# Local and global value products regrouped in a fused attention and feed-forward kernel on one core

## The chip, the cores and the metric

One core of one Trainium2 chip. The time is device microseconds of one execution; the kernel before has a median of 1009.82 us over 3 runs (1008.92 to 1010.57).

## The reference

Two stages. The first is attention with 8 batches, 8 heads, 512 local and 32 global positions and head size 64; local positions see the global ones and a window of 32 to each side, global positions see all. The second is a feed-forward layer on the 4608 tokens of 512 channels, 2048 wide inside.

```python
k_all = concat([k_g, k_l]); v_all = concat([v_g, v_l])
s_g = scale * q_g @ k_all.T
out_g = softmax(s_g) @ v_all
s_ll = where(abs(i - j) <= 32, scale * q_l @ k_l.T, -1e9)
s_lg = scale * q_l @ k_g.T
out_l = softmax(concat([s_lg, s_ll])) @ concat([v_g, v_l])
x = concat([out_g, out_l])            # tokens x 512
h = maximum(x @ w_in, 0)
out = (s * h * h + b) @ w_out
```

All inputs are float32.

## The kernel before

The work is laid out in steps `j` (the loop at L582). A step takes one head of one half of a batch (256 local rows): 16 steps are one batch, 128 steps are all heads. Each half batch gives one tile of 256 tokens with all 512 channels; the feed-forward layer of a tile is 8 steps `m`, each with two blocks of 128 inner channels, and runs 10 steps behind the attention (`m = j - LAG`). Tile 16, the last, holds the global rows of all batches, which travel through a DRAM tile `xg_d`.

Most products are made in float32r (one pass of the array) from operands split into a high and a low part: ScalarE casts the high part, VectorE or GpSimd subtracts it to get the low part. A plain float32 matmul takes no split; it shows in the trace as two records, each with its own weight load.

In a step, in TensorE's order: the scores of head `j` (`scores`, four matmuls at L351 and one for the global queries at L363); in odd steps the local value products of the two heads `j-3` and `j-2` (`pv`, L318, float32, the two heads in the lower and upper 64 columns of the array); the first feed-forward product of step `m` (`ffn_in`, 24 matmuls at L493); in some steps the global value product (`g_pv`, L443); the second feed-forward product of step `m-1` (`ffn_out`, 12 matmuls at L528), with the transposes of the global probabilities (`g_transposes`, L417) between its halves where they are due. At the last step of a tile's eight (`m % 8 == 7`) the next tile is split into `xs` (`x_split`, L464 on ScalarE and L465 on VectorE), behind that step's first product; `xs` has one buffer, and `ffn_in` of the next step reads it, channel block by channel block, each with the products high x high, weight-high x x-low and weight-low x x-high.

The local path of a head: scores, softmax on VectorE and ScalarE (L207, L214, L217 to L223), copies to `two` (L384), a DMA transpose issued by SyncE (L386), a copy `join` on ScalarE one step later (L394), then `pv`, whose result ScalarE copies to the tile `x` (L325). `pt`, which `join` writes, and `rv`, the values, have two buffers each, one per pair of heads.

The global path of four heads (half the heads of a batch, `g`): `g_softmax` at step 16b+12 or 16b+16; three steps later the transposes, whose result is split by ScalarE (L421) and VectorE (L422) into `pg`; V comes in two loads of 320 KB (`g_load`, L427), is split by ScalarE (L434) and GpSimd (L435) into `vsg`; then two products `g_pv` for two heads each, one and three steps behind the transposes, of 10 matmuls with 64 output columns (32 queries, high and low) and 128 moving columns (64 values, high and low). ScalarE copies (L447) and VectorE adds (L448, L451) the parts.

From step 18 on (`ORDERED`), TensorE, ScalarE and VectorE run in the order of the program text (`manual_schedule`); GpSimd, SyncE's queue and everything before step 18 are ordered by the framework's scheduler. The 8 first head pairs (steps 0 to 15) take another path with float32 products throughout, beside the loading and splitting of the weights (`weight_chunk`), which use the buffers `pg` and `vsg` too. The eight banks of PSUM have the tags s, g, t, o, h (two), acc0 and acc1; `pv` uses o, `g_pv` t.

Of the kernel before, what the change touches and what calls it, by code (L numbers as in the profile page):

```python
# [10 lines left out]
F32 = mybir.dt.float32  # L11
F32R = mybir.dt.float32r
# [9 lines left out]
P = 128  # L22
# [22 lines left out]
NF = 16  # L45
# [8 lines left out]
X_ACT = lambda i: i >= 4  # L54
G_AT = (12, 16)
G_TR = 3
G_LD = (0, 2)
G_PV = (1, 3)
GL_POOL = lambda m: False
K_POOL = lambda j: True  # L60

# [1 line left out]
def f32(ap):  # L63
    return ap.bitcast(F32)
# [3 lines left out]
def window_attention_then_ffn(ctx: ExitStack, tc: tile.TileContext, qd, qp, qg, kw, vw, vg, w_in, w_out, sv, bv, out):  # L68
# [214 lines left out]
    def chunks(j):  # L283
        b, hf, h = slot(j)
        o = 0
        for blk in range(2):
            for c in range(2):
                c0, q0, n = CHUNKS[hf, blk][c]
                yield blk, c, c0, q0, n, slice(o, o + n)
                o += n  # L290
# [18 lines left out]
            list(p_transposes(j))  # L309
            nc.scalar.copy(out=pt[:, n, 0:NC], in_=st_.pop(("pst", j)))  # L310

    def pv(i):
        pt, rv = st_.pop(("ptp", i)), st_.pop(("rvp", i))
        p_o = ps.tile([P, 2, 2, P], F32, tag="o", name=f"ps_op{i}")
        for blk, c, c0, q0, n, o in sorted(chunks(2 * i), key=lambda x: (x[0], -x[1])):
            v = (2 * blk + c) * D
            for k in range(2):
                nc.tensor.matmul(  # L318
                    p_o[64 * k:64 * k + 64, 0, blk, q0:q0 + n], lhsT=rv[:, k, v:v + D],
                    rhs=pt[:, k, o] if i < NF // 2 else pt[:, k, 2 * blk + c, q0:q0 + n],  # L320
                    start=(c == 1), stop=(c == 0),
                )
        x_out = x_tile(2 * i)[:, i % 4, :].rearrange("p (k q) -> p k q", k=2)
        if X_ACT(i):
            nc.scalar.copy(out=x_out, in_=p_o[:, 0])  # L325
        else:
            nc.vector.tensor_copy(out=x_out, in_=p_o[:, 0])

    def qg_load(b):
        rqg = sb.tile([P, 264], F32, tag="xr", name=f"rqg{b}", bufs=1)[:, 0:H * SG]  # L330
# [78 lines left out]

    def g_transposes(b, g):  # L410
        sg = st_["sg", b, g]
        pg = st_["pg", b, g] = sb.tile([P, 5, 4, 2, SG], F32R, tag="pg", name=f"pg{b}_{g}", bufs=1)
        for c0, c1, tag in ((0, 4, "t"), (4, 5, "o")):
            p_t = ps.tile([P, 4, P], F32, tag=tag, name=f"ps_tg{b}_{g}_{c0}")
            for c in range(c0, c1):
                s0 = min(c * P, SGW - P)
                nc.tensor.transpose(out=p_t[:, c - c0, :], in_=sg[:, s0:s0 + P], identity=ident)  # L417
            v = p_t[:, 0:c1 - c0].rearrange("p c (h q) -> p (c h) q", h=4)
            ph, pl = (pg[:, c0:c1, :, i, :].rearrange("p c h q -> p (c h) q") for i in range(2))
            with tc.high_priority():  # L420
                nc.scalar.copy(out=ph, in_=v)  # L421
                nc.vector.tensor_sub(out=pl, in0=v, in1=f32(ph))  # L422
            yield

    def g_load(b, h):
        rv = st_["rvg", b, h] = sb.tile([P, 10 * D], F32, tag="rvg", name=f"rvg{b}_{h}", bufs=1)
        nc.sync.dma_start(rv, vg[b, h // 2])  # L427

    def g_split(b, h):
        rv = st_.pop(("rvg", b, h))  # L430
        vs = sb.tile([P, 2, 5, 2, D], F32R, tag="vsg", name=f"vsg{b}_{h}", bufs=1)
        for i in range(2):
            rv5 = rv[:, 5 * D * i:5 * D * (i + 1)].rearrange("p (c d) -> p c d", d=D)
            nc.scalar.copy(out=vs[:, i, :, 0, :], in_=rv5)  # L434
            nc.gpsimd.tensor_sub(out=vs[:, i, :, 1, :], in0=rv5, in1=f32(vs[:, i, :, 0, :]))  # L435
        st_["vsg", b, h] = vs

    def g_pv(b, h):
        pg, vs = st_["pg", b, h // 4], st_.pop(("vsg", b, h))
        p_g = ps.tile([P, 512], F32, tag="t", name=f"ps_og{b}_{h}")  # L440
        for i in range(2):
            for c in range(5):
                nc.tensor.matmul(  # L443
                    p_g[0:64, i * P:(i + 1) * P], lhsT=pg[:, c, h % 4 + i], rhs=vs[:, i, c], start=(c == 0), stop=(c == 4),
                )
        t = sb.tile([32, 2 * P + 40], F32, tag="og", name=f"og{b}_{h}", bufs=1)[:, 0:2 * P]
        nc.scalar.copy(out=t, in_=p_g[32:64, 0:2 * P])  # L447
        nc.vector.tensor_add(out=t, in0=p_g[0:32, 0:2 * P], in1=t)  # L448
        xr = sb.tile([P, 264], F32, tag="xr", name=f"xr{b}_{h}", bufs=1)[0:32, 0:2 * D]
        t = t.rearrange("q (h a d) -> q h a d", h=2, a=2)  # L450
        nc.vector.tensor_add(out=xr.rearrange("q (h d) -> q h d", h=2), in0=t[:, :, 0], in1=t[:, :, 1])  # L451
        nc.sync.dma_start(xg_d[b * SG:(b + 1) * SG, h * D:(h + 2) * D], xr)


    NT = 17
# [28 lines left out]
    def ffn_in(m, then):  # L484
        t, pr = m // 8, m % 8
        xs = xs_[t]
        p_h = ps.tile([P, 2, HALF], F32, tag="h", name=f"ps_h{m}", bufs=2)
        for k in range(2):
            f = 2 * pr + k
            n = 0  # L490
            for c in range(4):
                for a, e in ((0, 0), (0, 1), (1, 0)):
                    nc.tensor.matmul(  # L493
                        p_h[:, k], lhsT=wi[f][:, a, c, :], rhs=xs[:, e, c, :],
                        start=(n == 0), stop=(n == 11),
                    )
                    n += 1
# [49 lines left out]

    ENGINES = {getattr(mybir.EngineType, e) for e in ("PE", "Activation", "DVE")}
    NM = NT * 8
    early, extra, turns = defaultdict(list), defaultdict(list), {}  # L550
    for b in range(B):
        for g in range(2):
            s0 = 16 * b + G_AT[g]
            early[s0].append(lambda b=b, g=g: g_softmax(b, g))
            turns[s0 + G_TR] = g_transposes(b, g)
            for i in range(2):
                h = 4 * g + 2 * i
                early[s0 + G_TR + G_LD[i] - 1].append(lambda b=b, h=h: g_load(b, h))
                early[s0 + G_TR + G_LD[i]].append(lambda b=b, h=h: g_split(b, h))
                extra[s0 + G_TR + G_PV[i]].append(lambda b=b, h=h: g_pv(b, h))  # L560

    def pick(pair, split_one):
        def run(j):
# [18 lines left out]
    for j in range(NM + LAG + 2):  # L582
        if j == ORDERED:
            fixed.enter_context(tc.manual_schedule(engines=ENGINES))
        sp(j + 1)
        if j + 4 < NF:
            ld(j + 4)
        if j + 2 >= NF:
            ld(j + 2)
        if NF <= j < NS and j % 2 == 0:  # L590
            v_load(j // 2)
        for _ in range(CHUNKS_AT[j] if j < len(CHUNKS_AT) else 0):
            weight_chunk(chunk)
            chunk += 1
        if j < NS:
            b1 = j // 16 + 1
            if j % 16 == 14 and b1 < B:
                qg_load(b1)
            sc(j)
            if j % 16 == 15 and NF <= j + 1 < NS:  # L600
                qg_split(b1)
        tr(j - 1)
        pvs(j - 2)
        if NF <= j - 3 < NS and j % 2:
            pv((j - 3) // 2)
# [10 lines left out]
        then = extra.pop(j, [])  # L616
# [16 lines left out]
    assert chunk == 16 and not extra and not early  # L633


# [73 lines left out]
```

## Time and profile before

| | |
|---|---|
| median of 3 runs | 1009.82 us |
| the profiled execution's own time | 1010.45 us |
| its span, first to last instruction | 1008.0 us |
| TensorE busy | 969.8 us, 96% |
| ScalarE busy | 744.2 us, 74% |
| VectorE busy | 688.1 us, 68% |
| GpSimd busy | 274.7 us, 27% |
| mean granted TensorE clock | 0.977 |

A profile row names the line, the engine, the operation and its tiles (out<-in), the part of the array used (rows*columns), the shape that is streamed, the count, and after the bar the busy time, the mean duration of one, and the idle time of the engine before them with what ended it. PE is TensorE's matmuls, PEld its weight loads, DVE VectorE, ACT ScalarE, POOL GpSimd, SP SyncE. Matmuls are pipelined: a bar lasts longer than the distance to the next one's start.

### The profile page before, as it was taken

The page shows a single profiled execution, that of the slowest core. Times are in us where ns is not written, and L with a number is a line of the kernel's source. Part 1 is how long each engine was busy: PE and PEld are TensorE (multiplying, and loading weights), DVE is VectorE, ACT ScalarE, POOL GpSimd, SP SyncE. Part 2 cuts the span into 40 slices and gives each one's busy share as a digit, 9 for nine tenths or more (in the row PEclk, how much of TensorE's full clock was granted, in tenths as well). Part 3 has the DMA queues.
Part 4 walks back from the last instruction along what each step waited for, and adds up shares of the span by engine and source line. Part 5 has one row for each costly group of instructions (what it writes and reads, how often), then busy time and mean ns, then how long its engine had stood idle before and what let it go on. Part 6 is the DMA issues. An engine that isn't in the chain of part 4 may idle for free.

```text
span 1008.0 us, 19973 instructions
## 1 busy us (share of the span) xinstructions
PE 969.8 (96%) x7060; PEld 861.2 (85%) x7060; DVE 688.1 (68%) x2092; ACT 744.2 (74%) x1618; POOL 274.7 (27%) x309
## 2 busy tenths in 40 slices
PE   6879999999999999999999999999999999999996
PEld 2468889998899888998999889998999889999895
DVE  5999866776767767777767767777767777753321
ACT  5987787778888787878877787787878787853221
POOL 1011332233323342233323342233323232211000
PEclk8769999999999999999999999999999999999998
DMA  8953254444544454444444454445544454331000
GB/s 323 349 185 99 67 137 109 114 105 120 126 112 100 104 137 107 112 110 122 123 114 101 98 143 99 118 105 132 119 115 102 120 120 88 84 60 36 12 21 21
DMA packets 179627, 115.07 MB, mean 114 GB/s; under 512 B 124744, under 2 KB 166728, under 8 KB 179528
## 3 DMA queue, kind: packets, MB, share of 16 engines
q1 hardware_dynamic: 179240, 112.76, 43.4%
q8 instruction: 55, 0.90, 0.4%
q10 hardware_dynamic: 288, 1.05, 0.4%
q14 instruction: 44, 0.36, 0.1%
HBM read 74.97 MB, written 9.44 MB: 84 GB/s over the span
## 4 chain that ended last, share of the span: by engine, by line
PE 48%; ACT 17%; DVE 10%; issue 2%; DVEq 0%; ACTq 0%
PE acc L528 21%; PE ps_h L493 20%; ACT sm L214 3%; DVE r L502 3%; PE ps_op L318 3%; ACT ptp L394 3%; ACT g L509 3%; PE ps_s L351 2%; ACT kq L191 2%; DVE two L384 1%; DVE xs L465 1%; ACT kq L193 1%; ACT tg L371 1%; PE ps_og L443 1%; ACT vsg L434 1%
## 5 line engine op out<-in xcount | busy, mean ns | idle before, releaser
L493 PE MATMUL ps_h<-xs,w 128*128 128x256 f32 x3264 | 420.9, 284 | 8.3 <-DVE xs L465 6.0
L493 PEld LDWEIGHTS ps_h<-xs,w 128*128 128x128 f32 x3264 | 397.7, 190 | 20.7 <-DVE xs L465 8.0
L528 PE MATMUL acc<-w,g 128*128 128x512 f32 x1632 | 403.3, 395 | 0.0
L528 PEld LDWEIGHTS acc<-w,g 128*128 128x128 f32 x1632 | 295.0, 188 | 57.4 <-issue 0.5
L192 POOL TENSOR_TENSOR kq<-rk,kq 64x416 fp32r<-64x416 f32 x112 | 125.3, 1119 | 550.7 <-ACT kq L191 537.5
L509 ACT ACTIVATE g<-r,b_t 128x512 fp32r<-128x512 f32 x136 | 98.4, 724 | 126.5 <-DVE r L502 126.5
L510 DVE SCALAR_TENSOR_TENSOR g<-r,b_t,g 128x512 fp32r<-128x512 f32 x136 | 102.1, 751 | 102.9 <-ACT g L509 102.9
L394 ACT COPY ptp<-turned 128x1024 int16<-128x1024 int16 x112 | 152.5, 1362 | 1.7 <-DMA turned<-two 1.7
L502 DVE SCALAR_TENSOR_TENSOR r<-ps_h,s_t,r 128x512 f32<-128x512 f32 x136 | 101.3, 745 | 68.0 <-ACT r L501 66.1
L214 ACT ACTIVATE sm<-sm,nm 128x224 f32<-128x224 f32 (+1 forms) x256 | 117.7, 461 | 3.1 <-DVE nm L207 1.1
L501 ACT ACTIVATE r<-ps_h 128x512 f32<-128x512 f32 x136 | 81.4, 599 | 47.4 <-PE ps_h L493 45.0
L384 DVE COPY two<-sm 128x256 int16<-128x256 int16 x448 | 100.5, 287 | 0.0
L194 POOL TENSOR_TENSOR kq<-rq,kq 128x256 fp32r<-128x256 f32 x112 | 84.4, 753 | 8.8
L435 POOL TENSOR_TENSOR vsg<-rvg,vsg 128x320 fp32r<-128x320 f32 x64 | 56.5, 904 | 89.2 <-ACT vsg L434 89.2
L207 DVE CUSTOM_DVE_ANT_0 sm<-ps_s,mask 128x192 f32<-128x192 f32 (+1 forms) x224 | 74.2, 368 | 7.0 <-PE ps_s L351 6.8
L351 PEld LDWEIGHTS ps_s<-kq 128*128 128x128 f32 x448 | 71.7, 189 | 7.0 <-DVE nm L207 0.2
L351 PE MATMUL ps_s<-kq 128*128 128x192 f32 (+1 forms) x448 | 77.7, 265 | 0.0
L217 DVE TENSOR_SCALAR ss<-ss 128x2 f32<-128x2 f32 (+1 forms) x120 | 37.4, 312 | 45.6 <-ACT sm L214 45.5
L223 DVE TENSOR_SCALAR sm<-sm,ss 128x192 f32<-128x192 f32 (+1 forms) x224 | 65.7, 336 | 3.9
L318 PE MATMUL ps_op<-ptp,rvp 128*64 128x128 f32 (+2 forms) x1024 | 66.4, 266 | 1.5 <-ACT ptp L310 1.4
L318 PEld LDWEIGHTS ps_op<-ptp,rvp 128*64 128x64 f32 x1024 | 53.3, 141 | 13.3 <-ACT ptp L310 3.6
L372 DVE TENSOR_TENSOR sg<-ps_g,tg 32x256 f32<-32x256 f32 (+1 forms) x112 | 48.2, 431 | 20.7 <-ACT tg L371 17.3
(68 smaller groups left out, 803.9 us busy)
## 6 DMA issues: line engine op xcount, KB each, us to landing
rvp<-in_vw SPq DMA_DIRECT2D x64, 256.0 KB, 2.9
rq<-in_qd SPq DMA_DIRECT2D x112, 128.0 KB, 2.3
rk<-in_kw SPq DMA_DIRECT2D x56, 208.0 KB, 2.4
rvg<-in_vg SPq DMA_DIRECT2D x32, 320.0 KB, 3.0
out<-o SPq DMA_DIRECT2D x34, 256.0 KB, 3.0
wst<-in_w_in SPq DMA_DIRECT2D x15, 512.0 KB, 6.1
wst<-in_w_out SPq DMA_DIRECT2D x15, 512.0 KB, 6.7
turned<-two SPq DMA_TRANSPOSE x112, 3.1
```

The lines of the kernel that those rows point to most:

```text
L192: (nc.gpsimd if K_POOL(j) else nc.vector).tensor_sub(out=ks[p1:p1 + 64], in0=rk[p0:p0 + 64], in1=f32(ks[p0:p0 + 64]))
L194: nc.gpsimd.tensor_sub(out=qs[:, 1, :], in0=rq, in1=f32(qs[:, 0, :]))
L214: nc.scalar.activation(out=p, in_=p, func=AF.Exp, bias=nm[:, n:n + 1], scale=-1.0, accum_out=ss[:, n:n + 1],)
L318: nc.tensor.matmul(p_o[64 * k:64 * k + 64, 0, blk, q0:q0 + n], lhsT=rv[:, k, v:v + D], rhs=pt[:, k, o] if i < NF // 2 else pt[:, k, 2 * bl ...
L351: nc.tensor.matmul(p_s[:, cols], lhsT=qs[:, a, blk * P:(blk + 1) * P], rhs=ks[:, cols], start=(a == 0), stop=(a == 1),)
L384: nc.vector.tensor_copy(out=two[:, 2 * blk + c], in_=sm[:, :, c0:c0 + P])
L394: nc.scalar.copy(out=pt.bitcast(I16).rearrange("p c (q h) -> p c h q", h=2), in_=st_.pop(("turned", j)))
L493: nc.tensor.matmul(p_h[:, k], lhsT=wi[f][:, a, c, :], rhs=xs[:, e, c, :], start=(n == 0), stop=(n == 11),)
L502: nc.vector.scalar_tensor_tensor(out=r, in0=p_h, scalar=s_t, in1=r, op0=ALU.mult, op1=ALU.mult)
L509: nc.scalar.activation(out=g[:, 0], in_=r, func=AF.Identity, bias=b_t)
L510: nc.vector.scalar_tensor_tensor(out=g[:, 1], in0=r, scalar=b_t, in1=f32(g[:, 0]), op0=ALU.add, op1=ALU.subtract,)
L528: nc.tensor.matmul(oacc[t][i], lhsT=g[:, a, k, i * P:(i + 1) * P], rhs=wo[f][:, e, :], start=(pr == 0 and n == 0), stop=(pr == 7 and n == 5),)
```

## The change

Local value products: `pv` takes two pairs of heads at once, at every fourth step (`j % 4 == 1`), into the two halves of one PSUM bank, with one copy of 128x512 behind them; the V loads of two pairs go out together at `j % 4 == 2`. Global value products: V and the probabilities are no longer split; one load of 640 KB for four heads at step 16b+14 or 16b+18, into the buffer `vsg`; one product for four heads, three steps later and directly behind `pv`, as 20 float32 matmuls with 32 output columns and 64 moving columns, each head at its own 32 columns of the array; one copy by ScalarE and one store to `xg_d`. In a tile's first feed-forward step the first of the two blocks takes all 8 products with the high part of x ahead of the 4 with the low part.

```diff
-G_LD = (0, 2)
-G_PV = (1, 3)
+G_LD = 2
+G_PV = 5
...
-    def pv(i):
-        pt, rv = st_.pop(("ptp", i)), st_.pop(("rvp", i))
+    def pv(i, n=1):
         p_o = ps.tile([P, 2, 2, P], F32, tag="o", name=f"ps_op{i}")
+        for u in range(n):
+            pt, rv = st_.pop(("ptp", i + u)), st_.pop(("rvp", i + u))
+            for blk, c, c0, q0, w, o in sorted(chunks(2 * i), key=lambda x: (x[0], -x[1])):
+                v = (2 * blk + c) * D
+                for k in range(2):
+                    nc.tensor.matmul(
+                        p_o[64 * k:64 * k + 64, u, blk, q0:q0 + w], lhsT=rv[:, k, v:v + D],
+                        rhs=pt[:, k, o] if i < NF // 2 else pt[:, k, 2 * blk + c, q0:q0 + w],
+                        start=(c == 1), stop=(c == 0),
+                    )
+        x_out = x_tile(2 * i)[:, i % 4:i % 4 + n, :].rearrange("p u (k q) -> p u k q", k=2)
         if X_ACT(i):
-            nc.scalar.copy(out=x_out, in_=p_o[:, 0])
+            nc.scalar.copy(out=x_out, in_=p_o[:, 0:n])
...
     def g_transposes(b, g):
-        pg = st_["pg", b, g] = sb.tile([P, 5, 4, 2, SG], F32R, tag="pg", name=f"pg{b}_{g}", bufs=1)
+        pg = sb.tile([P, 1280], F32, tag="pg", name=f"pg{b}_{g}", bufs=1)[:, 0:5 * P].rearrange("p (c r) -> p c r", c=5)
...
-            with tc.high_priority():
-                nc.scalar.copy(out=ph, in_=v)
-                nc.vector.tensor_sub(out=pl, in0=v, in1=f32(ph))
+            nc.scalar.copy(out=pg[:, c0:c1], in_=p_t[:, 0:c1 - c0])
...
+    def g_load(b, g):
+        rv = st_["rvg", b, g] = sb.tile([P, 4, 5, D], F32, tag="vsg", name=f"rvg{b}_{g}", bufs=1)
+        nc.sync.dma_start(rv.rearrange("p h c d -> p (h c d)"), vg[b, g])
+
+    def g_pv(b, g):
+        pg, rv = st_.pop(("pg", b, g)), st_.pop(("rvg", b, g))
+        p_g = ps.tile([P, 512], F32, tag="t", name=f"ps_og{b}_{g}")
+        for c in range(5):
+            for n in range(4):
+                m = slice(SG * n, SG * n + SG)
+                nc.tensor.matmul(p_g[m, 0:D], lhsT=pg[:, c, m], rhs=rv[:, n, c], start=(c == 0), stop=(c == 4))
+        og = sb.tile([P, P + 40], F32, tag="og", name=f"og{b}_{g}", bufs=1)[:, 0:D]
+        nc.scalar.copy(out=og, in_=p_g[:, 0:D])
+        rows = xg_d[b * SG:(b + 1) * SG, 4 * g * D:(4 * g + 4) * D]
+        nc.sync.dma_start(rows.rearrange("q (h d) -> h q d", h=4), og)
...
-            for c in range(4):
-                for a, e in ((0, 0), (0, 1), (1, 0)):
...
+            order = [(c, a, e) for c in range(4) for a, e in ((0, 0), (0, 1), (1, 0))]
+            if pr == 0 and k == 0:
+                order.sort(key=lambda x: x[2])
...
-        if NF <= j < NS and j % 2 == 0:
-            v_load(j // 2)
+        if NF <= j < NS and j % 4 == 2:
+            for i in (j // 2 - 1, j // 2):
+                v_load(i)
...
-        if NF <= j - 3 < NS and j % 2:
-            pv((j - 3) // 2)
+        if NF <= j - 5 < NS and j % 4 == 1:
+            pv((j - 5) // 2, 2)
+        for fn in gpv.pop(j, []):
+            fn()
```

The functions `g_split` (the casts and subtractions of V) and the additions of `g_pv` are gone; the host lays V out for four heads at a time.

## Rows read from the trace of the kernel before

**Rows 1.** The page: busy time and instructions of each engine; granted clock in 40 slices.

```profile
PE 969.8 (96%) x7060; PEld 861.2 (85%) x7060; DVE 688.1 (68%) x2092; ACT 744.2 (74%) x1618; POOL 274.7 (27%) x309
...
PEclk8769999999999999999999999999999999999998
```

**Rows 2.** Busy time of each engine in one period, with granted clock and DMA.

```profile
344.28:456.30 112.02, 111.00 (x835) 100.30 (x834) 80.19 (x266) 89.49 (x199) 37.90 (x42) 1.00 0.46 114
```

**Rows 3.** TensorE's timeline, plain step and pv step: start us, us, instruction.

```profile
415.22 0.48 PE L351 MATMUL ps_s<-kq 128*128 128x224 f32 x3
...
421.33 0.47 PE L351 MATMUL ps_s<-kq 128*128 128x224 f32 x3
...
421.95 0.94 PE L318 MATMUL ps_op<-ptp,rvp 128*64 128x128 f32 x16
422.82 3.07 PE L493 MATMUL ps_h<-xs,w 128*128 128x256 f32 x24
...
428.50 0.47 PE L351 MATMUL ps_s<-kq 128*128 128x224 f32 x3
```

**Rows 4.** Groups of instructions by shape, 380 to 890 us.

```profile
L318 PEld LDWEIGHTS ps_op<-ptp,rvp 128*64 128x64 f32 x592 | 28.7, 136 | 4.3
...
L318 PE MATMUL ps_op<-ptp,rvp 128*64 128x96 f32 x148 | 12.4, 246 | 0.0
...
L318 PE MATMUL ps_op<-ptp,rvp 128*64 128x64 f32 x148 | 10.5, 220 | 0.0
```

**Rows 5.** TensorE's timeline around a tile's first step.

```profile
442.40 0.25 PE L351 MATMUL ps_s<-kq 128*128 128x192 f32 x1
...
445.75 0.76 PE L443 MATMUL ps_og<-vsg,pg 128*64 128x128 f32 x10
...
449.15 0.25 PE L351 MATMUL ps_s<-kq 128*128 128x192 f32 x1
...
456.30 0.25 PE L351 MATMUL ps_s<-kq 128*128 128x192 f32 x1
...
456.95 0.38 PE L493 MATMUL ps_h<-xs,w 128*128 128x256 f32 x1
458.40 2.96 PE L493 MATMUL ps_h<-xs,w 128*128 128x256 f32 x23 [1.06 <-DVE xs L465]
...
464.59 0.25 PE L351 MATMUL ps_s<-kq 128*128 128x192 f32 x1
```

**Rows 6.** Timeline of ScalarE and VectorE ahead of that step.

```profile
455.56 0.82 ACT L434 CAST vsg<-rvg 128x320 fp32r<-128x320 f32 x2
...
456.27 1.14 ACT L464 CAST xs<-x 128x512 fp32r<-128x512 f32 x2
...
456.93 2.01 DVE L465 TENSOR_TENSOR xs<-x,xs 128x512 fp32r<-128x512 f32 x2 [0.81 <-ACT xs L464]
```

**Rows 7.** Group of first-layer matmuls, whole span; then from the waits, TensorE for VectorE.

```profile
L493 PE MATMUL ps_h<-xs,w 128*128 128x256 f32 x3264 | 420.9, 284 | 8.3 <-DVE xs L465 6.0 <-ACT xs L464 1.8 <-DVE xs L479 0.5
...
PE ps_og L443 <- DVE pg L422: 1.6, 6, 0.4
```

**Rows 8.** Groups of ScalarE's instructions by shape, whole span.

```profile
L434 ACT CAST vsg<-rvg 128x320 fp32r<-128x320 f32 x64 | 26.2, 461 | 1.5 <-DVE w L165 1.5
...
L325 ACT COPY x<-ps_op 128x256 f32<-128x256 f32 x60 | 22.4, 373 | 3.2 <-PE ps_op L318 1.8
...
L536 ACT COPY o<-acc 128x512 f32<-128x512 f32 x34 | 19.6, 578 | 8.9 <-DVE g L510 6.0 <-PE acc L528 2.9
...
L447 ACT COPY og<-ps_og 32x256 f32<-32x256 f32 x32 | 11.3, 354 | 12.3 <-PE ps_og L443 12.1 <-DVE sm L223 0.2
```

**Rows 9.** DMA issues: count, KB each, median us to landing.

```profile
rvp<-in_vw SPq DMA_DIRECT2D x64, 256.0 KB, 2.9
...
rvg<-in_vg SPq DMA_DIRECT2D x32, 320.0 KB, 3.0
```

**Rows 10.** Waits of SyncE's queue: total us, times, longest.

```profile
SPq L258 <- PE ps_op L318: 71.3, 48, 7.4
```

More of the change, by code (lines that the diff above doesn't have):

```diff
@@ L310, in transposes32 @@
             nc.scalar.copy(out=pt[:, n, 0:NC], in_=st_.pop(("pst", j)))
-    def pv(i):
-        pt, rv = st_.pop(("ptp", i)), st_.pop(("rvp", i))
+    def pv(i, n=1):
         p_o = ps.tile([P, 2, 2, P], F32, tag="o", name=f"ps_op{i}")
[L315 to L323, printed above, removed]
+        for u in range(n):
[9 more added lines that the diff above has]
+        x_out = x_tile(2 * i)[:, i % 4:i % 4 + n, :].rearrange("p u (k q) -> p u k q", k=2)
         if X_ACT(i):
-            nc.scalar.copy(out=x_out, in_=p_o[:, 0])
+            nc.scalar.copy(out=x_out, in_=p_o[:, 0:n])
         else:
-            nc.vector.tensor_copy(out=x_out, in_=p_o[:, 0])
+            nc.vector.tensor_copy(out=x_out, in_=p_o[:, 0:n])
     def qg_load(b):
@@ L411, in g_transposes @@
         sg = st_["sg", b, g]
-        pg = st_["pg", b, g] = sb.tile([P, 5, 4, 2, SG], F32R, tag="pg", name=f"pg{b}_{g}", bufs=1)
+        pg = sb.tile([P, 1280], F32, tag="pg", name=f"pg{b}_{g}", bufs=1)[:, 0:5 * P].rearrange("p (c r) -> p c r", c=5)
+        st_["pg", b, g] = pg
         for c0, c1, tag in ((0, 4, "t"), (4, 5, "o")):
@@ L417, in g_transposes @@
                 nc.tensor.transpose(out=p_t[:, c - c0, :], in_=sg[:, s0:s0 + P], identity=ident)
-            v = p_t[:, 0:c1 - c0].rearrange("p c (h q) -> p (c h) q", h=4)
-            ph, pl = (pg[:, c0:c1, :, i, :].rearrange("p c h q -> p (c h) q") for i in range(2))
-            with tc.high_priority():
-                nc.scalar.copy(out=ph, in_=v)
-                nc.vector.tensor_sub(out=pl, in0=v, in1=f32(ph))
-            yield
-    def g_load(b, h):
-        rv = st_["rvg", b, h] = sb.tile([P, 10 * D], F32, tag="rvg", name=f"rvg{b}_{h}", bufs=1)
-        nc.sync.dma_start(rv, vg[b, h // 2])
@@ L429, in g_split @@
[L429 to L452, printed above, removed]
@@ L489, in ffn_in @@
             f = 2 * pr + k
-            n = 0
-            for c in range(4):
-                for a, e in ((0, 0), (0, 1), (1, 0)):
[L493 to L497, printed above, removed]
+            order = [(c, a, e) for c in range(4) for a, e in ((0, 0), (0, 1), (1, 0))]
+            if pr == 0 and k == 0:
+                order.sort(key=lambda x: x[2])
+            for n, (c, a, e) in enumerate(order):
+                nc.tensor.matmul(
+                    p_h[:, k], lhsT=wi[f][:, a, c, :], rhs=xs[:, e, c, :], start=(n == 0), stop=(n == 11),
+                )
         for fn in then:
@@ L549, in window_attention_then_ffn @@
     NM = NT * 8
-    early, extra, turns = defaultdict(list), defaultdict(list), {}
+    early, gpv, turns = defaultdict(list), defaultdict(list), {}
     for b in range(B):
@@ L555, in window_attention_then_ffn @@
             turns[s0 + G_TR] = g_transposes(b, g)
[L556 to L560, printed above, removed]
+            early[s0 + G_LD].append(lambda b=b, g=g: g_load(b, g))
+            gpv[s0 + G_PV].append(lambda b=b, g=g: g_pv(b, g))
     def pick(pair, split_one):
@@ L615, in window_attention_then_ffn @@
             x_split(0)
-        then = extra.pop(j, [])
+        then = []
         if 0 <= m < NM:
@@ L632, in window_attention_then_ffn @@
     fixed.close()
-    assert chunk == 16 and not extra and not early
+    assert chunk == 16 and not gpv and not early
 def kernel(**inputs):
@@ L684 @@
     vg = _np.stack(vg, axis=2)
-    vg = vg.reshape(B, H // 2, 2, 5, P, D).transpose(0, 1, 4, 2, 3, 5)
-    vg = _np.ascontiguousarray(vg).reshape(B, H // 2, P, 10 * D)
+    vg = vg.reshape(B, 2, 4, 5, P, D).transpose(0, 1, 4, 2, 3, 5)
+    vg = _np.ascontiguousarray(vg).reshape(B, 2, P, 20 * D)
     w_in = a["moe_w_in"].reshape(DM // P, P, DF // P, P).transpose(2, 1, 0, 3)
```

## The prediction

> **What bounds the kernel now.** I read the page's busy shares first. TensorE is busy for 96% of the span, ScalarE 74%, VectorE 68%, and from the fourth of the 40 slices on the granted clock stands at 0.9 or more, its upper level of 2.4 GHz [rows 1]. A share over a whole span mixes stages, so next comes one period of the steady part: 16 steps, which is one batch, take 112.02 us, and TensorE is busy in 111.00 of them, ScalarE in 89.49 [rows 2]. The reader is to see that almost nothing is left but TensorE's own instructions, so a TensorE instruction taken away there is time taken away. Then TensorE's timeline gives prices as differences of step lengths, from the first score matmul (L351) of one step to that of the next. A plain step lasts 421.33 - 415.22 = 6.11 us; one with local value products (L318) 428.50 - 421.33 = 7.17 [rows 3]; one with a global value product (L443) 449.15 - 442.40 = 6.75 [rows 5]. The step from 456.30 to 464.59 has the same work as that last one and takes 8.29: its first-layer matmuls stood 1.06 us waiting for VectorE's low parts xs of the new tile [rows 5]. Last, the groups of instructions and the waits say how often such things happen [rows 4, 6, 7].
>
> **Edit 1, local value products for four heads at a time.** Before, 16 matmul records of L318 come every second step; after, 32 every fourth. Columns and passes are the same, so only the cost of a visit is saved: 28 visits go (heads 16 to 127 make 56 pairs, now 28 groups). A visit costs 7.17 - 6.11 = 1.06 us. How much of that is streaming? A record of 96 columns lasts 246 ns and one of 64 lasts 220 [rows 4], so 26/32 = 0.81 ns a column. A head pair is 8 matmuls, each recorded twice (two passes), so 16 records; two of them must run side by side, one per head (one after the other, 1664 columns would be 1.35 us, and all 16 are through in 0.94 [rows 3]), so there are 8 pairs with 2 x (128+96+128+64) = 832 columns: 0.68 us. The rest, 0.38 us, is the change between the array's layouts on the way in and out. The least that can be saved is what lies outside the stretch from the first L318 to the first L493 (422.82 - 421.95 = 0.87 us [rows 3]): 1.06 - 0.87 = 0.19. Bounds for a removed visit are thus 0.19 and 0.38. I take 0.35, near the upper one, because that stretch also contains the first weight load and the drain at its end. 28 x 0.35 = **9.8 us** (5.3 to 10.6).
>
> What comes with it: ScalarE makes 28 copies of 128x512 out of PSUM in place of 56 of 128x256: 373 ns each before, and 578 ns for the nearest row of the new size, the output copy L536 [rows 8], so 4.7 us less on ScalarE. The join copy that reuses the first pair's buffer is behind this copy in ScalarE's order, so it gains no wait of its own. The v loads move by up to two steps and go out in twos; both wait for the same step's products. SyncE already stands at such loads 48 times for 71.3 us, up to 7.4 [rows 10], and behind them stand the q and k loads and the transposes. A load lands in 2.9 us [rows 9] and is wanted three steps later, some 18 us, so I cost this at nothing; the cover is that distance, and without it the landing time would show.
>
> **Edit 2, global value products in float32.** Before, each of the 32 products lengthens its step by 6.75 - 6.11 = 0.64 us: 20.5 us. After there are 16, each of 20 matmuls with 32 output columns and 64 moving columns, so with two passes 40 records. If four column groups run side by side as two do in L318, it is 10 x 64 x 0.81 ns = 0.52 us. It stands directly behind the local products, so the way in from the 128-column layout is paid already, but going from 64 to 32 columns is a change no row shows: between 0 and 0.38 us, and I take half of a 0.35 visit, 0.17. That makes 0.69 x 16 = 11.0 and saves **9.5 us**. The ends are 0.52 (saves 12.2) and, with every record behind its own weight load of 136 ns [rows 4], 5.6 (loses 69): the second is rival E.
> The rule that speaks against this is in the Trainium skill, "TensorEngine Tiling (Array Packing)", Key Properties: changing the tiling mode, not merely the tile, drains the engine. The trace agrees for 128 to 64 columns (0.38 us above the streaming) and shows nothing for 64 to 32. By the rule the full 0.38 would be paid, 0.90 x 16 = 14.4, and the sum would come out 3.4 us higher, at 981, inside the forecast's own range.
>
> Also gone is the wait of these products for VectorE's pg low parts: 1.6 us of idle in 6 waits [rows 7]; as the bar of the matmul before lasts 0.28 us [rows 7] where its neighbour starts after 0.12 (23 of them span 2.96 us [rows 5], so (2.96 - 0.28)/22), each costs 0.16 more, together **2.6 us**. On ScalarE the casts of V (L434, 26.2 us) and the copies L447 (11.3) go [rows 8], and 16 small copies come (5.7 us if each costs what one of L447 does, 354 ns). With edit 1 that is 37 us of relief on an engine that in a period had 22.5 us free [rows 2]; VectorE and GpSimd only lose work. I count none of it, since TensorE sets the end. The g load becomes one of 640 KB in place of two of 320 KB, and shares its step with two v loads: 1152 KB. Even one after the other at the landing times of today (2.9 us for 256 KB, 3.0 for 320 [rows 9]) they are there after 12 us, within the three steps until use. A transpose that queues behind them lands later than today; its join has two steps before the products want it, though ScalarE waits there in order.
>
> **Edit 3, high parts first in a tile's first step.** The order defers the first use of a low part by 4 to 8 matmuls of 0.12 us. In the step shown, ScalarE's casts of V (456.27 - 455.56 = 0.71 us) are directly before the casts to xs, and VectorE's subtractions behind these end at 458.94, while TensorE wanted them from 456.95 on [rows 5, 6]. Now those V casts are gone, and the step before is longer on TensorE by the merged products (1.06 - 0.35 = 0.71 local, 0.69 global) and the step before that shorter by 0.64. So the data comes 0.7 us earlier at least, is wanted 0.7 us later, and its late half 0.9 us later still: more than the 1.5 us missing. The stall goes: 8.29 - 6.75 = 1.5 us in each of the six whole periods, 9.0, and 0.7 at the last tile (0.5 of idle behind L479 [rows 7] and a bar's 0.2): **9.7 us**. Late next would be TensorE's own score matmuls behind ScalarE's splits, which have a step to spare.
>
> **Sum.** 9.8 + 9.5 + 2.6 + 9.7 = 31.6 us off the profiled execution's 1010.45: 978.9. That execution lies 0.6 above the median of the runs, so 978. The schedule of the first 120 us is made anew and may move by a few us either way; I take 0.
>
> **Rivals.**
> B, only two column groups run at once: 20 pairs of 64 columns, 1.04 + 0.17 = 1.21 us x 16 = 19.4, 8.4 more: 986. For it: no row shows four side by side. Against it: the two that L318 shows need nothing special. In the Trainium skill, "TensorE: Matmul & The Clock Gate", Back-to-back issue gap, gives an issue floor of about 25 ns for each matmul; by that, 40 records would be 1.0 us, almost the same. No row here is dense enough to bear it out.
> C, the tile's stall stays (something else delays xs: a transfer behind the 1152 KB, or the doubled copy ahead of it): 9.0 more, 987. For it: ScalarE and VectorE wait for each other in every step. Against it: the 1.4 us of shift above.
> D, no overlap at all: 40 x 52 ns + 0.17 = 2.25 us x 16 = 36, 25 more: 1003.
> E, the other side: each of the 40 records is held by its own weight load, because a load into one of four narrow column groups isn't hidden behind the others. At 136 ns: 5.6 us x 16 = 89, 78 more: 1056. It decides from 62 ns a record on (all other savings, 22.1, and the 20.5 of before are eaten up at 2.66 us a product). Against it: in L318 the loads are as long (136 ns [rows 4]) and 16 records still end within 0.94 us [rows 3].
>
> **The numbers.** Forecast (A) 0.63, B 0.18, C 0.09, D 0.04, E 0.06. About 0.2% (2 us) is what a measurement of this kernel tells from no change. A to D are all faster by more: 0.94; of E a sixth could fall within 0.2% (0.01), the rest is slower (0.05). A's own range is 972 to 986: below, 0.38 a visit (0.8), no switch (2.7) and some 2 from the start; above, 0.19 a visit (4.5) and a full switch (3.4). To reach B and C the range goes to 990, and below to 970; D and E, 0.10, are left out, as are the tails of A.
>
> **What would show it.** Right: steps with local products every fourth, some 7.84 us plus 0.7 where a global one follows; plain steps still 6.1; no idle of L493 behind xs; one period near 107 us. Edit 1 is wrong if a merged step takes over 8.1 us; edit 2 if the new product takes over 1 us (B) or 2 (D, E); edit 3 if L493 still waits. The whole is wrong if plain steps grow, as ScalarE or the transposes would then have become the bound.

## The result and the profile after

| | before | after |
|---|---|---|
| median | 1010.2 us (4 runs, 1008.92 to 1011.03) | 980.39 us (4 runs, 978.63 to 982.35) |
| profiled execution | 1010.45 us | 982.35 us |
| its span | 1008.0 us | 980.5 us |

The ratio is 0.9712, with a 95% interval of 0.9698 to 0.9725: 2.9% faster. The forecast was 978, with a range of 970 to 990. The lines that answer to [rows 1], and the shares of the chain of work that ended last, of the kernel after:

```profile
PE 948.3 (97%) x7380; PEld 846.3 (86%) x7380; DVE 651.0 (66%) x1996; ACT 714.6 (73%) x1510; POOL 217.4 (22%) x245
...
PE 91%; DVE 3%; DMA 3%; ACT 1%; SPq 0%; issue 0%; POOL 0%; POOLq 0%; ACTq 0%
```

And the same chain of the kernel before, which the prediction does not use:

```profile
PE 48%; ACT 17%; DVE 10%; issue 2%; DVEq 0%; ACTq 0%
```

The reader is to see how little the busy shares tell: TensorE goes from 96% to 97%, yet its share of the chain goes from 48% to 91%. These are shares of the span, and the chain of before is followed back only to 226 us, so its shares add up to 77%; of that part TensorE has 62%, ScalarE and VectorE 35%. One period says it more clearly. Summed over the chain's pieces from 456.30 to 568.23 us, TensorE has 47.8 us, ScalarE 37.8 and VectorE 21.3; in the period ahead of it, that of [rows 2], 86.2, 15.9 and 9.5. In the period of after that is shown below, the chain is TensorE's alone. In the kernel before, the chain leaves TensorE at 436.25 us and comes back to it at 476.08; among the pieces between are several that edit 2 takes away, the casts of V (L434), the split of pg (L421, L422) and the additions (L448). Start us, us, what:

```profile
435.34 0.89 PE ps_op L318 x16
436.25 0.39 ACT tg L371
...
439.61 0.67 ACT vsg L434 x2
...
442.32 0.50 ACT pg L421 x2
...
449.81 0.33 DVE og L448
...
455.71 0.67 ACT vsg L434 x2
456.38 0.53 ACT xs L464
...
456.93 2.01 DVE xs L465 x2
...
475.33 0.61 DVE pg L422
...
476.08 0.79 PE ps_og L443 x10
```

One period of 16 steps, which answers to [rows 2] (start and end, length, then busy time of PE, PEld, DVE, ACT and POOL, granted clock, DMA share, GB/s):

```profile
439.96:547.48 107.52, 107.52 (x876) 98.28 (x875) 75.93 (x255) 85.89 (x183) 30.30 (x33) 1.00 0.51 119
```

The period fell from 112.02 to 107.52 us at the same granted clock, and TensorE no longer waits in it at all. TensorE's timeline of the kernel after, which answers to [rows 3, 5]: a step with the four heads' products and the global product, then a tile's first step (start us, us, instruction):

```profile
439.96 0.25 PE L352 MATMUL ps_s<-kq 128*128 128x192 f32 x1
...
440.59 1.66 PE L319 MATMUL ps_op<-ptp,rvp 128*64 128x128 f32 x32
442.17 0.77 PE L433 MATMUL ps_og<-rvg,pg 128*32 128x64 f32 x40
442.87 3.07 PE L479 MATMUL ps_h<-xs,w 128*128 128x256 f32 x24
...
448.52 0.25 PE L352 MATMUL ps_s<-kq 128*128 128x192 f32 x1
...
449.06 2.98 PE L479 MATMUL ps_h<-xs,w 128*128 128x256 f32 x24
...
454.64 0.25 PE L352 MATMUL ps_s<-kq 128*128 128x192 f32 x1
```

The merged step lasts 448.52 - 439.96 = 8.56 us, and the tile's first step 454.64 - 448.52 = 6.12, the length of a plain one: the first-layer matmuls stand in one unbroken bar where [rows 5] had a gap of 1.06 us. Over all steps, one with four heads' products and no global product lasts 7.89 on average and one with both 8.58, so the global product costs about 0.69. From the groups of instructions of the kernel after, the lines that answer to [rows 7, 8] (busy us, mean ns | idle before, with what ended it):

```profile
L479 PE MATMUL ps_h<-xs,w 128*128 128x256 f32 x3264 | 412.7, 281 | 1.5 <-DVE nm L207 1.5
...
L433 PE MATMUL ps_og<-rvg,pg 128*32 128x64 f32 x640 | 12.2, 221 | 0.0
...
L326 ACT COPY x<-ps_op 128x512 f32<-128x512 f32 x28 | 16.5, 588 | 2.9 <-PE ps_op L319 1.5
...
L450 DVE TENSOR_TENSOR xs<-x,xs 128x512 fp32r<-128x512 f32 x32 | 20.7, 687 | 22.5 <-ACT xs L449 22.5
```

TensorE's idle time behind xs is gone (8.3 us of idle before, 6.0 of it for VectorE's part). VectorE's timeline has the two subtractions that this step needs:

```profile
447.81 1.29 DVE L450 TENSOR_TENSOR xs<-x,xs 128x512 fp32r<-128x512 f32 x2 [0.44 <-ACT xs L449]
```

They end at 449.10, when TensorE has just begun the products of the tile (449.06); in [rows 6] the same two took 2.01 us and ended 2 us after TensorE wanted them.

**Where the time went.** Step 19 begins at 131.29 us after and at 127.47 before, so the start lost 3.8 us. From there to the end it is 849.2 us against 880.5: 31.3 less, where the prediction's sum was 31.6. Both are read from the profiled executions, and that of the kernel after is the slowest of its four runs.

### The profile page after: what moved, and what is told of

Same layout as the page of the kernel before. It is cut to its first block, busy times and chain, and to the rows that moved or that the text cites. A ratio compares the mean times of both kernels' runs of the same rounds, so it can differ in the third digit from the quotient of the medians.

```text
span 980.5 us, 20198 instructions
## 1 busy us (share of the span) xinstructions
PE 948.3 (97%) x7380; PEld 846.3 (86%) x7380; DVE 651.0 (66%) x1996; ACT 714.6 (73%) x1510; POOL 217.4 (22%) x245
## 4 chain that ended last, share of the span: by engine, by line
PE 91%; DVE 3%; DMA 3%; ACT 1%; SPq 0%; issue 0%; POOL 0%; POOLq 0%; ACTq 0%
PE ps_h L479 39%; PE acc L512 38%; PE ps_op L319 5%; PE ps_s L352 5%; PE ps_g L364 1%; PE ps_og L433 1%; DMA wst<-in_w_in 1%; PE ps_tg L419 1%; DMA b_t<-in_bv 1%; DVE we L161 1%; DMA wst<-in_w_out 1%; DVE wst L160 1%; DMA rkp<-in_kw 1%; DVE w L165 0%; DVE we L157 0%
## 5 line engine op out<-in xcount | busy, mean ns | idle before, releaser
L479 PE MATMUL ps_h<-xs,w 128*128 128x256 f32 x3264 | 412.7, 281 | 1.5 <-DVE nm L207 1.5
L319 PE MATMUL ps_op<-ptp,rvp 128*64 128x128 f32 (+2 forms) x1024 | 61.4, 266 | 2.5 <-ACT ptp L310 2.3
L191 ACT CAST kq<-rk 64x416 fp32r<-64x416 f32 x112 | 59.8, 534 | 2.0 <-PE ps_s L352 0.7
```

The source lines that it names most:

```text
L319: nc.tensor.matmul(p_o[64 * k:64 * k + 64, u, blk, q0:q0 + w], lhsT=rv[:, k, v:v + D], rhs=pt[:, k, o] if i < NF // 2 else pt[:, k, 2 * bl ...
L479: nc.tensor.matmul(p_h[:, k], lhsT=wi[f][:, a, c, :], rhs=xs[:, e, c, :], start=(n == 0), stop=(n == 11),)
```

## The experiments

### Each edit alone, and the third undone

**The change without edit 3** (label `e_order_old`).

```diff
-            if pr == 0 and k == 0:
-                order.sort(key=lambda x: x[2])
```

> The changed kernel with edit 3 undone. Theory (the casts of V and the uneven steps had moved xs, the order adds nothing in the steady part): in the trace of the changed kernel the second low half of xs lands 0.04 us after the first matmul of the tile at most, and the old order wants it only 0.8 us after, so no stall comes back but the last tile's 0.7 us; time within 2 us of the changed kernel, about 981. Rival (the order carries the stall, as the prediction booked it): about 1.3 to 1.5 us at six tiles and 0.7 at the last, about 9 us more, 989 or 990.

Measured: 979.12 us (4 runs), ratio 0.97 (0.9684 to 0.9716). The steps stay 6.12, 7.89 and 8.58 us. The stall of the tile's first step did not come back; only the last tile waits for xs, 0.5 us:

```profile
L477 PE MATMUL ps_h<-xs,w 128*128 128x256 f32 x3264 | 413.2, 282 | 2.0 <-DVE nm L207 1.5 <-DVE xs L464 0.5
```

Step 19 begins at 127.18. So edit 3 is not what ended the stall in the steady part, and the late start came with it.

**Edit 3 alone** (label `e_order_only`): the kernel before with those two lines and the list `order`.

> The kernel before with edit 3 alone. Theory: the first low half comes 1.39 us (or 0.67) after the tile's first matmul could start and the second 1.97; with the new order they are wanted 0.94 and 1.17 us after it, so 0.8 us of the 1.3 (or 1.1) stay: 0.4 x 6 = 2.4 us gained, and 0.7 at the last tile, about 1007. Rival (the order alone removes the stall): 9.7 us gained, about 1000.5.

Measured: 1008.34 us (10 runs), ratio 0.9991 (0.9982 to 1.0001), where some 1007 had been expected. The stalled step shrank from 8.28 to 7.92 us on average over the six periods, but the step behind it grew from 7.74 to 8.01 and the next from 7.21 to 7.32, together by as much, and the period stayed:

```profile
344.14:456.21 112.07, 111.30 (x835) 100.32 (x834) 80.29 (x266) 89.47 (x199) 37.34 (x42) 1.00 0.47 114
```

(The first of the two has the transposes and two heads' products, the second the global product that waits for pg.) What TensorE no longer waits at one place it loses at another. That is the first sign that TensorE alone does not set these 112 us.

**Edit 1 alone** (label `e_pv_only`): the kernel before with the new `pv`, its V loads and its steps.

```diff
-        if NF <= j < NS and j % 2 == 0:
-            v_load(j // 2)
+        if NF <= j < NS and j % 4 == 2:
+            for i in (j // 2 - 1, j // 2):
+                v_load(i)
...
-            pv((j - 3) // 2)
+            pv((j - 5) // 2, 2)
```

> The kernel before with edit 1 alone. Theory: 28 visits less at 0.33 us (steps of 7.89 in place of 7.17 + 0.72) are 9.2 us, and the tile's stall falls by about 0.5 us at six tiles since the step ahead of it is 0.7 us longer: 12 us gained, about 998. Rival (a longer visit holds ScalarE and VectorE up and comes back as waits in the plain steps): plain steps over 6.2 us and less than 5 us gained.

Measured: 1010.4 us (10 runs), ratio 1.0011 (1.0002 to 1.002): nothing gained, a miss by 12 us. TensorE's steps are exactly those planned (plain 6.12, with products 7.89), but its waits grew. One fence each for the period, the group of first-layer matmuls, and the timeline of a tile's first step:

```profile
342.64:454.72 112.08, 109.42 (x835) 99.74 (x834) 80.70 (x268) 89.13 (x195) 37.53 (x41) 1.00 0.46 114
```

```profile
L494 PE MATMUL ps_h<-xs,w 128*128 128x256 f32 x3264 | 420.9, 284 | 12.7 <-DVE xs L466 6.7 <-ACT xs L465 5.5 <-DVE xs L480 0.5
```

```profile
343.95 0.38 PE L494 MATMUL ps_h<-xs,w 128*128 128x256 f32 x1 [0.61 <-ACT xs L465]
345.38 2.96 PE L494 MATMUL ps_h<-xs,w 128*128 128x256 f32 x23 [1.05 <-DVE xs L466]
```

TensorE's busy time in a period fell by 1.6 us (111.00 to 109.42) and the period by nothing. TensorE comes earlier to the tile's first step and waits there for the same data: first for ScalarE's casts, then for VectorE's subtractions. Two steps later it waits 0.9 to 1.0 us for pg, where it had waited 0.2 to 0.4. In the second half of the kernel the whole loss stands at the tile's first step, which then lasts 10.4 to 10.8 us, and the periods that begin with such a step last 112.4 and 112.7.

**Edit 2 alone** (label `e_gpv_only`): the change with the old `pv` at every second step and the old order of products.

> The kernel before with edit 2 alone. Theory: the global products cost 16 x 0.69 in place of 32 x 0.65 (9.8 us gained), their wait for the low parts goes (2.6), and so does the stall at the tile's first step, without the new order (9.0): 21 us gained, about 989. Rival (the stall needs the new order): 12.4 gained, about 998.

Measured: 987.94 us (4 runs), ratio 0.9789 (0.9774 to 0.9803): 21 us. TensorE again waits for xs only at the last tile, 0.5 us. So edit 2 alone ends the stall; and edit 1, worth nothing on the kernel before, is worth 987.94 - 979.12 = 8.8 us on top of edit 2. So edit 1 does not give its saving back by itself; on the kernel before something else takes it.

### The price of the new global product

**Heads outermost** (label `e_gpv_serial`): the same 20 matmuls, those of one head one after the other.

```diff
-        for c in range(5):
-            for n in range(4):
-                m = slice(SG * n, SG * n + SG)
+        for n in range(4):
+            m = slice(SG * n, SG * n + SG)
+            for c in range(5):
```

> The changed kernel with the global product's loops turned round: all five blocks of one head, then the next head, so that neighbours in the order share their 32 columns. Theory (the speed comes from neighbours on four different column groups running side by side): 40 records one after the other, 40 x 53 ns and the change of layout, 2.2 us in place of 0.69, 24 us more, about 1005. Rival (the array runs at most two column groups or takes them in any order): 0.7 to 1.2 us, at most 8 us more.

Measured in a single run: 999.16 us; the step lasts 9.66 us, so the product costs 9.66 - 7.89 = 1.77, against 0.69 side by side. The 40 records start at distances of about 41 ns, if the 0.14 us found below is taken off first: (1.77 - 0.14) / 40. That is less than the 52 ns that rival D took for records one after another, and lies between the two expectations.

**Products issued twice** (label `e_gpv_twice`): `for c in [0, 1, 2, 3, 4] * 2`.

> The changed kernel with the 20 matmuls of each global product issued twice into the same sums (the second round starts them anew). The second round pays streaming alone: Theory (four side by side): 0.53 us more in each of the 13 steps that hold both products, so that 0.16 us of the 0.69 is the change from 64 to 32 columns; about 989. Rival (the change costs nothing and the records run 17 ns apart): 0.69 more.

Measured in a single run: 989.96 us; the merged step lasts 9.136 us on average where it had 8.581, so a further round of 40 records costs 0.555 us, 14 ns a record, and what is left of 0.69 for the switch of layout is 0.14.

**Products in a step of their own** (label `e_gpv_apart`): `G_PV = 6` in place of 5, one step behind the local products.

> The changed kernel with the global product one step later, in a step without local products. Theory (a visit from the 128-column layout costs 0.33 us each way together, and the place behind the local products saves that): a step of 6.12 + 0.53 + 0.33 to 0.5 = 7.0 to 7.15 us, and steps with four heads of 7.89; 3 to 5 us more in all. Rival (it is the change to 32 columns alone that costs): 6.12 + 0.69 = 6.81, time as the changed kernel's.

Measured in a single run: 984.19 us; the step lasts 6.98 us, so the product alone costs 0.86, of which 0.31 (0.86 less the 0.55 of its records) is the visit. Behind the local products it saves 0.17 us each time.

### The late start

**The priority given back** (label `e_hp`): the change drops a `tc.high_priority()` around the copies of `g_transposes`, which could alter the order that the framework's scheduler makes of the start. It stands again.

> The changed kernel with the high priority of the copies behind the global transposes put back, which can only move the order before step 18. Theory (the changed kernel reaches step 19 at 131.3 us where the kernel before did at 127.5, because the scheduler made another order of the first 120 us): the start moves by some us and the steady part by nothing; step 19 between 126 and 133 us, time 976 to 982. Rival (the start varies from run to run, with the same order): step 19 falls anywhere in the spread of the runs, and the median stays within 1 us of the changed kernel's.

Measured: 981.39 us (4 runs), ratio 0.9714 (0.9698 to 0.9731); step 19 begins at 130.95. The priority is not the cause.

**Edit 3 for the last tile only** (label `e_order_last`).

```diff
-            if pr == 0 and k == 0:
+            if t == NT - 1 and pr == 0 and k == 0:
```

> The changed kernel with the new order kept for the last tile alone. Theory (the new order buys 0.7 us at the last tile and nothing elsewhere, and made the scheduler reach step 19 about 4 us later, which the run without it had back): step 19 near 127.2 us as without edit 3, no wait at the last tile, about 978.4 and 1 to 2 us under the changed kernel. Rival (the later start is not the order's): as the changed kernel, 980.4.

Measured: 978.51 us (4 runs, 978.27 to 979.04), ratio 0.9689 (0.9674 to 0.9703). Step 19 begins at 127.30 and the last tile no longer waits for xs:

```profile
L479 PE MATMUL ps_h<-xs,w 128*128 128x256 f32 x3264 | 413.4, 282 | 1.4 <-DVE nm L207 1.4
```

Its median is 1.9 us below that of the change; the ranges touch (the change's fastest run took 978.63), so the gain is small against the scatter. All five kernels that have the three edits in the early tiles too (the change, `e_hp` and the three of the section before) begin step 19 between 130.6 and 132.1 us; all others, edit 3 alone among them, begin it between 126.1 and 127.5, each read from one profiled execution. So the late start comes with edit 3 in the early tiles beside the other two, by the order that the scheduler makes of the start; edit 3 beside only one of them was not run. In that order TensorE waits 2.1 us for a join of the start that is not awaited in `e_order_old` or `e_order_last`:

```profile
78.09 0.93 PE L319 MATMUL ps_op<-ptp,rvp 128*64 128x128 f32 x14 [2.11 <-ACT ptp L310]
```

### What sets the 112 us

**Casts of V moved to GpSimd** (label `e_pv_pool`): edit 1 alone, with `nc.scalar.copy` of V replaced by `nc.gpsimd.tensor_copy`.

> Edit 1 alone, as in the run that gained nothing, but with the casts of V moved from ScalarE to GpSimd; TensorE's work is the same. Theory (the period of 112 us before was set by the loop of ScalarE and VectorE, not by TensorE, so a visit saved on TensorE came back as waits): ScalarE is freed of 3.7 us in each batch; the tile's stall and the wait for the global probabilities fall by some 0.8 us each, six times or more, and about 8 to 12 us of the saving show: 998 to 1002. Rival (something else gave the saving back, such as the longer visit itself or the loads in twos): 1008 to 1012.

Measured: 1014.0 us (4 runs), ratio 1.0041 (1.0026 to 1.0056): slower, a miss. The period grew to 112.86 us. First the groups of VectorE's copies to `two` from 340 to 900 us, here and then in `e_pv_only`; then this kernel's timeline with four such copies and what GpSimd does beside them, and four copies of `e_pv_only` without that neighbour:

```profile
L385 DVE COPY two<-sm 128x256 int16<-128x256 int16 x316 | 96.3, 367 | 0.0
```

```profile
L385 DVE COPY two<-sm 128x256 int16<-128x256 int16 x316 | 71.9, 291 | 0.0
```

```profile
446.37 2.25 DVE L385 COPY two<-sm 128x256 int16<-128x256 int16 x4
...
445.44 0.88 POOL L435 CAST vsg<-rvg 128x320 fp32r<-128x320 f32 x2
446.28 1.78 POOL L436 TENSOR_TENSOR vsg<-rvg,vsg 128x320 fp32r<-128x320 f32 x2
```

```profile
782.25 0.89 DVE L385 COPY two<-sm 128x256 int16<-128x256 int16 x4
```

VectorE's copies take 2.25 us for four beside GpSimd's work and 0.89 without it; in this run, too, the four copies of the step before and of the step after take 0.88 and 0.89. In a period ScalarE's busy time fell from 89.1 to 86.1 us and VectorE's rose from 80.7 to 85.7: the relief of one was the load of the other. That leaves open which of the two the period hangs on, so the next run loads ScalarE alone.

**ScalarE loaded again** (label `e_act_load`): `e_order_old`, with 64 copies of 128x320 on ScalarE where the casts of V had stood; nobody reads them.

```diff
+    def load_act(b, g, i):
+        for n in range(2):
+            dead = sb.tile([P, 5, D], F32, tag="dead", name=f"dead{b}_{g}_{i}_{n}", bufs=1)
+            nc.scalar.copy(out=dead, in_=st_["held", b, g][:, 2 * i + n])
```

> Edits 1 and 2 (the old order of the first-layer products) with dead copies put on ScalarE where the casts of V stood: 64 copies of 128x320 whose results nobody reads, 27 us of ScalarE's time, and nothing else changed. Theory (edit 2 works through ScalarE for the larger part): waits come back at the tile's first step, 0.3 to 1.5 us in each period and more as the lag carries over; 983 to 990 where it was 979. Rival (edit 2 works through TensorE's shorter products alone and ScalarE has room): 981 at most.

Measured: 988.41 us (4 runs), ratio 0.9781 (0.9765 to 0.9798), so 0.0081 x 1009 = 8.2 us more than `e_order_old`. The group of the copies, and TensorE's timeline at a tile's first step:

```profile
L430 ACT COPY dead<-rvg 128x320 f32<-128x320 f32 x64 | 29.3, 459 | 1.8 <-DMA rvg<-in_vg 0.8
```

```profile
449.73 0.38 PE L482 MATMUL ps_h<-xs,w 128*128 128x256 f32 x1 [0.20 <-ACT xs L454]
450.46 2.96 PE L482 MATMUL ps_h<-xs,w 128*128 128x256 f32 x23 [0.34 <-DVE xs L455]
```

The stall is back at its old place, some 1.0 us a period there and 0.3 two steps later, with all of TensorE's work unchanged. But the period goes only from 107.5 to 108.9 us, although ScalarE is as busy in it as it was before (88.6 and 89.5 us):

```profile
448.84:557.72 108.88, 108.28 (x875) 98.37 (x874) 76.01 (x254) 88.60 (x192) 30.37 (x33) 1.00 0.49 117
```

So the casts of V on ScalarE are enough to make TensorE wait, and they are not all that made the 112 us: some 3 us of it came from other things that edit 2 takes away. One of them can be read from the subtractions of xs from 340 to 900 us, first in `e_pv_only`, then here, where GpSimd has no subtractions of V:

```profile
L466 DVE TENSOR_TENSOR xs<-x,xs 128x512 fp32r<-128x512 f32 x20 | 16.5, 863 | 15.1 <-ACT xs L465 15.1
```

```profile
L455 DVE TENSOR_TENSOR xs<-x,xs 128x512 fp32r<-128x512 f32 x22 | 14.2, 688 | 18.5 <-ACT xs L454 18.5
```

Between the two spans (987.1 and 977.3 us) lie 9.8 us: 8.0 of these stalls in six periods, 2.9 in a longer step 19, and 1.1 given back by an earlier start.

**Edit 1 without the splits of V** (label `e_pv_nosplit`): V is split for the first two heads only, and that split is used for all later ones, so the V of the later heads is left out of the global rows. The subtractions of V on GpSimd go with the casts.

```diff
+        if (b, h) != (0, 0):
+            st_["vsg", b, h] = st_["vs0"]
+            return
```

> Edit 1 alone, with V split only for the first pair of heads and that split used for all later ones: the V of the later heads is loaded but left out of the global rows. TensorE's instructions are the same as in the run with edit 1 alone; ScalarE loses 63 of its 64 casts' worth (26 us) and GpSimd its subtractions, which ran beside VectorE. Theory (the loop of ScalarE and VectorE set the period, so edit 1 had no effect until that loop was relieved): the waits at the tile's first step fall below 0.5 us and the saving of the 28 visits shows: 16 to 20 us under the run with edit 1 alone, 990 to 994. Rival (edit 1 itself gives its saving back): at most the tile's stall goes, 1000 to 1003, or nothing, 1010.

Measured: 1013.63 us (4 runs), ratio 1.0055 (1.0038 to 1.0072), far from the expected time. The steady part did as expected: the period and the group of first-layer matmuls are

```profile
373.74:483.22 109.49, 108.93 (x835) 99.62 (x834) 79.53 (x268) 86.57 (x186) 30.37 (x33) 1.00 0.43 105
```

```profile
L497 PE MATMUL ps_h<-xs,w 128*128 128x256 f32 x3264 | 417.0, 283 | 2.8 <-ACT xs L468 1.9 <-DVE xs L483 0.5 <-DVE xs L469 0.4
```

so 112.08 became 109.49 and the waits for xs fell from 12.7 to 2.8 us. Compared with `e_pv_only`, some 21 us were lost in five long steps between 126 and 216 us; without them the time would be about 993, inside the theory's range (an estimate). In these steps the loads that nobody reads go out early, SyncE's queue waits for earlier ones to land, and the DMA transposes behind them come late:

```profile
SPq L428 <- DMA rvg<-in_vg: 54.8, 29, 3.3
```

```profile
ACT ptp L395 <- DMA turned<-two: 22.3, 11, 5.0
```

That the one delays the other is read from these waits and was not tried by itself.

## Why the prediction was right, and where not

- **The size.** Forecast A held: 980.39 in a range of 970 to 990. From step 19 to the end the terms come out, by mean step lengths, as 28 visits x 0.31 us (8.8; forecast 9.8), 8.8 for the global products of that stretch (forecast 9.5 for all), 2.7 for the waits behind pg (forecast 2.6), 9.9 for those behind xs (forecast 9.7), and 0.9 that nobody forecast, a wait for VectorE's sg in step 19 that fell from 1.44 to 0.51 us: together 31.1 of the 31.3 measured. That the sum came so close is partly luck, as the next points show.
- **Edit 1's visit** was priced at 0.35 us. A step with four heads' products is 7.89 - 6.12 = 1.77 longer than a plain one, one with two heads' 1.04 on average, so a visit saved is 2 x 1.04 - 1.77 = 0.31; the product in a step of its own gives the same 0.31. The merged step that the prediction names as a sign, "some 7.84", is 7.17 + 0.71 = 7.88 by its own terms.
- **Edit 2's product** was priced at 0.69 (0.52 streaming, 0.17 switch) and took 0.69 (0.55 and 0.14). Rivals B, D and E fall with it: 40 records in 0.55 us need more than two column groups at once, and no record waits 136 ns for its own weight load. The match of the streaming is luck in part. It was priced at 52 ns a record and four at a time; if the 41 ns of heads outermost are what a record costs alone, it was 41 ns and about three at a time. The full switch of 0.38 us was not paid. The issue floor of about 25 ns that the Trainium skill gives, "TensorE: Matmul & The Clock Gate", Back-to-back issue gap, does not agree with records 14 ns apart; it does with matmul instructions of two records each, 28 ns apart.
- **The start** was taken as 0, with a few us either way, and cost 3.8 us in the profiled execution: the term that was mis-sized. That execution took 982.35 where the sum for it was 978.9. In the medians it costs less: 980.39 is 2.4 above the forecast, and `e_order_last`, which starts early, is 1.9 below it.
- **"I count none of it, since TensorE sets the end"** was wrong, and the total hid it. The relief of ScalarE and VectorE by edit 2 was the main thing. On the kernel before, TensorE loses 1.6 us of work a period by edit 1 and 0.4 of a stall by edit 3, and from step 34 on the period does not fall below 111.9 either time; without the splits of V it falls to 109.5; and with ScalarE loaded again a part of the stall returns. In the period of [rows 2] TensorE was busy for 111.00 us, and yet 25 us of the chain in it, and 59 in the next, run through ScalarE and VectorE; their lateness reached TensorE at xs, at every other tile, and at pg. The two limits lay so close together (112.0, and 110.1 for TensorE's steps without their waits of 1.5 and 0.4 for xs and pg) that step lengths and waits added up to the period, and the sum over them looked complete. The Trainium skill, "Perfetto Trace Analysis", Identifying the Most-Contended Engine, says to work first on the most-contended engine, with TensorE judged by its share of peak work and by its weight loads and not by its matmuls' busy time; the weight loads were busy for 85% of the span [rows 1], still ahead of ScalarE's 74%, and edit 1 alone, which works on TensorE, gained nothing.
- **Edit 3's 9.7 us** were booked on the wrong edit. The prediction named the right reasons (no casts of V ahead of the casts to xs, a later want), but both belong to edit 2 and the merged step; edit 2 alone ended the stall. The order itself was also mis-sized: it defers the first use of the four low parts by 7, 5, 3 and 1 matmuls and not by 4 to 8, so the late half is wanted 0.37 us later (3 x 0.12) and not 0.9; edit 3 alone shortened the stalled step by 0.37. In the change it is worth 0.8 us at the last tile (850.1 us from step 19 to the end without it, 849.25 in `e_order_last`), and the late start stands against it.
- **Rival C** (the stall stays) is what happens without edit 2's relief; its place was right, its mechanism (a transfer, the doubled copy) was not: both are in `e_order_old`, which has no stall but the last tile's.
- **Transposes later**, costed at nothing, are later: ScalarE waits for them 9 times for 7.0 us where it had waited 3 times for 1.7, and TensorE waited for none of it in the steady part, as foreseen.
- **The clock row** of [rows 1] stands at 0.8 in its last slice, not at 0.9 or more as the prediction reads it; no term rests on that.

What stays open: how the 3 us of the period that ScalarE's casts of V do not explain divide between GpSimd's subtractions beside VectorE's work, VectorE's and ScalarE's split of pg, and the additions of `g_pv`, since no run takes these away one by one (`e_pv_nosplit`, which keeps the last two, has 109.5 us, so the casts and GpSimd's subtractions together are most of it); and what in the scheduler's order makes the late start.

## What to carry to other kernels

An engine that is busy for 99% of a period need not set it: look at the chain that ended last over one period (here up to 59 of 112 us ran through other engines), and try whether the period shrinks when this engine alone loses work. Gains of edits do not add up when two limits lie 2% apart: the same edit was worth nothing alone and 8.8 us behind another, so each one is measured alone and undone. The waits of another engine in a period do not tell such cases apart: ScalarE waits 1.1 us for TensorE before and 0.4 after, as a wait names only the last link.

## What the runs showed of the hardware

- Matmuls into four groups of 32 columns stream side by side at 14 ns a record of 64 columns when neighbours in the order use different groups; with neighbours in the same group the same records take about 41 ns. "TensorEngine Tiling (Array Packing)" of the Trainium skill, Key Properties, says that different tiles can work in parallel, and both numbers agree.
- The change from groups of 64 columns to groups of 32 cost 0.14 us, less than half of the 0.31 us of a visit from the full width and back.
- VectorE's int16 copies went from 0.89 to 2.25 us for four while GpSimd cast and subtracted beside them, and its subtractions of xs took 863 ns each in `e_pv_only` and 688 in the runs without GpSimd's subtractions of V (`e_pv_nosplit`, `e_act_load`). "GPSIMD Engine Reference" of the Trainium skill, Key points, says that the two engines share their interfaces to SBUF and that VectorE's instructions with two SBUF inputs, or in a mode that uses both ports, suffer from it. The trace agrees that there is such a loss; which mode these copies ran in no row shows.
